# Pair 0's last two steps also with second layers of seven products, the change of form moved inside pair 0, its weight sets made first

## The chip, the cores and the metric

The kernel runs on one core of a Trainium2 chip. TensorE (PE) multiplies, VectorE (DVE) and ScalarE (ACT) read its results out of PSUM, GpSimd (POOL) works on SBUF alone, and SyncE (SP) issues most transfers. Each engine takes its own instructions strictly in the order of the program and waits for the others at semaphores. The metric is the time of one execution on the device in microseconds (us), the median of three runs.

## What is computed

The reference is a chain of a 2-D Fourier transform, a gated feed-forward layer, and a second feed-forward layer, "network two", which is where the change lies:

```python
def _moe2_ref(x, w_in, w_out):          # x: 12288 x 256, w_in: 256 x 2048, w_out: 2048 x 256
    h = x @ w_in
    g = h - np.tanh(h)
    return (g @ w_out).astype(np.float32)
```

## The kernel before

All products run in fp32r, with each operand split into a high part (a cast to fp32r, "hi") and a low part (the value minus its high part, "lo"). One product of a 128x128 weight block with 512 columns is three matmuls in a row (lines 395 to 397: high weights by high data, high weights by low data, low weights by high data).

Network two takes the tokens in 12 pairs (n) of 2x512 and w_in's columns in 8 steps (q) of 256; a step is written (n,q). Both layers of a step are 2x2 block products. The first layer is done with seven products instead of eight (operands `a11 a12 s1 s2 s3 s4 a22`, summed in banks `x`, `z`, `w`). Then come tanh, the subtraction, and the second layer. That layer has two forms. The whole form multiplies the four gated blocks 11, 12, 21, 22 by two halves of w_out, eight products (`WO`). The form of seven needs the same kind of sums on the gated data (`s1 s2 s3 s4`, made by DVE and POOL from `g11 g12 g22` and `x`) and of the weights (`W7`, seven blocks, a "set" for each q), but runs seven products: `a12 s4 a22` go straight into the output banks `o`, the others into a bank `k` whose sum is added into SBUF (`acc`).

`quad` writes a step with only whole forms; before, all of pair 0 goes through it. `step` writes a step of pairs 1 to 11, where q = 0, 1, 3, 4, 6, 7 have seven products and q = 2, 5 the whole form. How `step` orders its instructions depends on the two steps before it: form "c" if the last step was whole, "e" if the last was of seven and the one before it whole, "b" if both were of seven. The second layer of a step runs inside the next one or two steps, between their first-layer products. The low parts `a11`, `s2`, `s3`, `s4` and others are POOL's, and so are two of the sums (`+s2`: g22 - g11; `+s4`: g12 - g22).

Each step has four slots; `at(slot, ...)` puts side work into them and `fill` writes it out there. The side work around the change is: `weights2` (first-layer weight sets `TI` of pair 0 and `WO`), `seven` (the `W7` sets), `left2` (the next pair's left operands), `stream` (the later `TI`, reloaded from HBM). A `W7` set is made of one ACT cast of 384 columns, one POOL subtraction of 384 columns, four POOL subtractions of 128 (the first part), and, a few slots later, an ACT cast and a POOL subtraction of 512 columns (the second part).

Before, sets 0, 1, 3 are made in the last two steps of pair 0, set 4 in (1,2) and (1,3), set 6 in (1,5) and (1,6), set 7 in (1,6) and (1,7).

Of the kernel before, what the change touches and what calls it, by code (L numbers as in the profile page):

```python
# [375 lines left out]
NP = 12  # L376
# [30 lines left out]
class Kernel:  # L407
# [513 lines left out]
    def weights2(self, slot, q, pool, tag, bufs):  # L921
        a, b, out = [], [], []
        def load(to, pool, tag, bufs, i):
            def f():
                to.append(pool.tile([128, TOK], F32, tag=tag, name="wf", bufs=bufs))
                self.nc.sync.dma_start(out=to[-1], in_=self.wf[i])
            return f
        def ti():
            p, t = (self.p2a, f"TI{q}") if q < 4 else (self.w1, "T")
            self.TI[q] = p.tile([128, 2, 7, 128], F32R, tag=t, name="TI", bufs=1 if q < 4 else 4)  # L930
            f, g = self.quad_weights(self.p2a, self.TI[q])
            f(a[0])
            b.append(g)
            out.append(self.TI[q])
        def wo():
            p, t = (self.p2a, f"WO{q}") if q < 4 else (self.wvp, "wv")
            self.WO[q] = p.tile([128, 2, TOK], F32R, tag=t, name="WO", bufs=1 if q < 4 else 4)
            self.split(self.WO[q], b[1], self.V if q < 2 else self.G)
        def keep():
            self.nc.sync.dma_start(out=self.ti[q], in_=out[0].rearrange("p s k n -> p (s k n)").bitcast(F32))  # L940
        self.at(max(slot - 3, 16 * NP - 12), load(a, self.kp, "xt", 4, 4 + q))
        self.at(slot + 1, ti, None, None, None, lambda: b[0](None))
        self.at(16 * NP + ((5, 6, 10)[q] if q < 3 else 4 * q + 1), keep)
        self.at(slot + 4, load(b, pool, tag, bufs, 12 + q), None, wo)

    def seven(self, slot, q, pool, tag, bufs, src_pool, src_tag, src_bufs, t4):

        src, t = [], []
        def load():
            src.append(src_pool.tile([128, TOK], F32, tag=src_tag, name="wf", bufs=src_bufs))  # L950
            for to, at, n in ((0, 128, 128), (128, 0, 128), (256, 256, 256)):
                self.nc.sync.dma_start(out=src[0][:, to:to + n], in_=self.wf[12 + q, :, at:at + n])
        def first():
            self.W7[q] = pool.tile([128, 2, 7, 128], F32R, tag=tag, name="W7", bufs=bufs)
            f, g = self.quad_weights(t4(), self.W7[q])
            f(src[0])
            t.append(g)
        if q == 6:
            self.hook = first
        self.at(slot, *[first] * (q != 6), *[None] * (4 + (q == 6)), lambda: t[0](None))  # L960
        self.at(slot - (2 if q == 7 else 4), load)

# [13 lines left out]
    def sevens(self, n):  # L976

        return (0, 1, 3, 4, 6) if n == NP - 1 else (0, 1, 3, 4, 6, 7)

# [60 lines left out]

    def part(self, n, t, h, eng=None):

        if n == 0:
            a = self.room(self.p2b, "acc", "o", 7)
            (eng or self.V.tensor_copy)(a, self.C.pop((n, t, h)))
            return self.send(n, t, h, a)
# [13 lines left out]
    def whole_out(self, n, t, h):  # L1060

        if n == 0:
            return
        a = self.acc[n, t, h]
        self.G.tensor_add(a, a, self.acc[n, "t" if t else "s2"])
        self.send(n, t, h, a)

    def step(self, n, q):
# [26 lines left out]
        late = lambda *names: [p1["late"][k]() for k in names]  # L1095
        turn, end = (n, q) == (1, 0), (n, q) == (NP - 1, 7)
        new = lambda name: self.room(self.kp, "xt", name, 4)
# [5 lines left out]
        if two and self.last(p2["n"], p2["q"]) == p2["q"]:  # L1103
            g = group(p2, p3)
            k1, k2 = (lambda: self.apart(g, "s2")), (lambda *i: self.apart(g, "s3", *i))
        if 8 * n + q + 1 < 8 * NP:
            self.stream(8 * n + q + 1)
        self.odd ^= 1
        X, Z = self.bank(f"x{self.odd}", "x"), self.bank("z", "z")

        after = form == "b" and p1["form"] == "e" and (n, q) != (1, 5)
        if form == "b" and not after:
# [6 lines left out]
        if form == "b":  # L1119
            late("f22")  # L1120
            if (n, q) == (1, 5):
                self.hook()
            if after:
                late("L22", "s3")
            else:
                late("l22", "s3")
        elif form == "e":
            if (n, q) == (1, 1):
                late("f22", "L22", "c12", "g21")
            else:  # L1130
                late("l22", "c12", "f22", "g21")
        else:
            late("t21", "c12", "g21")
        A.copy(Z, X)  # L1134
        if form == "b":
            self.direct(p2, "s4")
            if (n, q) == (1, 2):
                self.direct(p2, "a22")
            if not after:
                self.direct(p1, "a22")  # L1140
            late("s1", "+s2", "hs1", "hs3", "c12", "t12")
        elif form == "c":
            self.whole(p1, "11", (1,))
            self.whole(p1, "22", (0,))
            late("t12", "h21", "g12")
            if q == 3 and n > 1:
                self.part(n - 1, 1, 1)
            late("l21", "h12")
        else:
            self.whole(p2, "21")  # L1150
            late("t12", "s3", "s1", "+s2")
            if end:
                late("hs1", "G12", "ls1")
            else:
                late("hs3", "ls3")
        P(Z, "a12")
        if form == "b":
            late("ls1", "ls3")
            if q == 1 and n > 1:
                C = self.C[n - 1, 0, 1]  # L1160
                V.tensor_add(C, C, self.acc[n - 1, "h"])
# [19 lines left out]
        if form == "b":  # L1181
            late("ha12", "+s4", "la12")
        if (n, q) == (1, 1):
            self.part(0, 1, 0)
            self.part(0, 1, 1, A.copy)
        self.fill()
        if form == "c":
            self.whole(p1, "22", (1,))
        elif form == "e":
            if (n, q) != (1, 1):  # L1190
                self.direct(p1, "a22")
            self.whole(p2, "12", (0,))
# [10 lines left out]
        add()  # L1203
        if q == 1 and n > 1:
            self.part(n - 1, 0, 0)
# [19 lines left out]
        elif form == "e":  # L1225
            self.whole(p2, "12", (1,))
        if (n, q) == (1, 1):
            self.part(0, 0, 0, A.copy)
        V.tensor_add(Z, Wb, s3)  # L1229
        if (n, q) == (1, 1):  # L1230
            self.part(0, 0, 1)
        if q == 1 and n > 1:
            self.outer(n - 1, 0, 1)
        if q == 0 and n > 1:
            self.part(n - 1, 1, 0)
# [255 lines left out]
```

## Time and profile before

| what | us |
|---|---|
| median of 3 runs (1611.01 to 1611.74) | 1611.54 |
| the profiled execution, its time | 1611.9 |
| its span, first to last instruction | 1610.1 |
| PE busy | 1595.5 |
| DVE, ACT, POOL busy | 1333.0, 1263.7, 1151.2 |

The span is what the trace shows of the execution; the rest of its time lies before the first and after the last instruction. Network two begins at 646.80 us, where the first product with `TI` starts. PE is drawn busy nearly all the time since matmuls overlap, so short waits show as starts that lie further apart than the matmuls alone would make them.

### The profile page before, as it was taken

How to read it: one execution, taken by the hardware profiler on the slowest of the kernel's cores; microseconds unless marked ns; L12 is line 12 of the kernel's file. 1: busy time of each engine (PE TensorE's matmuls, PEld its weight loads, DVE VectorE, ACT ScalarE, POOL GpSimd, SP SyncE). 2: the span in 40 equal slices, each digit the busy share in tenths (PEclk: the TensorE clock that was granted, in tenths of full speed). 3: DMA queues.
4: the chain of work that ended last, by engine and by line, in shares of the span. 5: the costliest groups of instructions: out<-in, count | busy, mean ns of one | idle time of the engine just before them, and what ended most of it. 6: DMA issues, size and time to landing. Idle time of an engine off the chain costs nothing.

```text
span 1610.1 us, 22467 instructions
## 1 busy us (share of the span) xinstructions
PE 1595.5 (99%) x7283; PEld 1305.2 (81%) x7283; DVE 1333.0 (83%) x2081; ACT 1263.7 (78%) x2444; POOL 1151.2 (71%) x962
## 2 busy tenths in 40 slices
PE   8999999999999999999999999999999999999998
PEld 7978888888888888787788888888888888888887
DVE  7987888888888887777787878887878787878787
ACT  5887777777777777788888888888787888888875
POOL 1156767656667676577887888787878787878764
PEclk9999999999999999999999999999999999999999
DMA  9630111112121112554142424343424242424240
GB/s 339 172 71 28 47 41 45 40 47 66 47 67 46 32 55 94 200 182 169 59 138 98 138 98 138 103 135 119 135 101 144 92 145 92 145 95 149 102 152 26
DMA packets 59349, 168.75 MB, mean 105 GB/s; under 512 B 6864, under 2 KB 15824, under 8 KB 59232
## 3 DMA queue, kind: packets, MB, share of 16 engines
q1 hardware_dynamic: 57648, 162.87, 29.7%
q0 software_dynamic: 1440, 4.46, 1.6%
q8 instruction: 57, 0.93, 0.2%
q14 instruction: 60, 0.49, 0.1%
q10 hardware_dynamic: 144, 0.00, 0.0%
HBM read 128.43 MB, written 38.86 MB: 104 GB/s over the span
## 4 chain that ended last, share of the span: by engine, by line
PE 93%; DVE 2%; DMA 1%; ACT 1%; POOL 1%; issue 1%; SPq 0%; DVEq 0%; ACTq 0%; POOLq 0%
PE o L395 11%; PE o L397 11%; PE o L396 11%; PE x L395 8%; PE x L397 8%; PE x L396 8%; PE w L395 4%; PE w L396 4%; PE w L397 4%; PE k L395 4%; PE k L396 4%; PE k L397 4%; PE z L395 2%; PE z L397 2%; PE z L396 2%; PE r L396 1%
## 5 line engine op out<-in xcount | busy, mean ns | idle before, releaser
L1094 POOL TENSOR_TENSOR s<-g,s 128x512 fp32r<-128x512 f32 x153 | 198.1, 1302 | 4.1 <-ACT s L1092 3.4
L696 POOL TENSOR_TENSOR s<-xk,s 128x512 fp32r<-128x512 f32 x94 | 125.1, 1332 | 87.8 <-ACT s L694 82.8
L696 POOL TENSOR_TENSOR a<-xk,a 128x512 fp32r<-128x512 f32 x70 | 92.3, 1327 | 121.2 <-ACT a L694 121.2
L396 PE MATMUL o<-m,wv 128*128 128x512 f32 x384 | 149.6, 390 | 0.1
L397 PE MATMUL o<-m,wv 128*128 128x512 f32 x384 | 149.5, 389 | 0.0
L395 PE MATMUL o<-m,wv 128*128 128x512 f32 x384 | 149.5, 389 | 0.0
L1094 POOL TENSOR_TENSOR a<-g,a 128x512 fp32r<-128x512 f32 x107 | 138.3, 1302 | 15.3 <-ACT g L1270 10.5
L1284 POOL TENSOR_TENSOR g<-g,g 128x512 f32<-128x512 f32 x65 | 84.3, 1297 | 53.4 <-DVE x L1283 42.5
L1087 ACT COPY s<-x 128x512 f32<-128x512 f32 x176 | 104.3, 593 | 22.6 <-PE x L397 19.6
L1083 ACT ACTIVATE c<-z 128x512 f32<-128x512 f32 x176 | 105.7, 601 | 10.1 <-DVE z L1229 8.2
L571 ACT ACTIVATE c<-z 128x512 f32<-128x512 f32 x112 | 67.3, 601 | 55.7 <-DVE z L660 54.9
L1243 DVE TENSOR_TENSOR z<-z,c 128x512 f32<-128x512 f32 x88 | 61.6, 700 | 52.1 <-ACT c L1083 49.5
L578 DVE TENSOR_TENSOR m<-z,m 128x512 fp32r<-128x512 f32 x112 | 76.8, 686 | 32.9 <-ACT m L576 32.9
L1092 ACT CAST s<-g 128x512 fp32r<-128x512 f32 x153 | 92.8, 623 | 5.6 <-DVE g L1283 5.6
L430 POOL TENSOR_TENSOR xr<-xt,xr 128x512 fp32r<-128x512 f32 x46 | 60.8, 1329 | 46.3 <-ACT xr L429 46.3
L576 ACT CAST m<-z 128x512 fp32r<-128x512 f32 x112 | 65.9, 589 | 27.9 <-DVE z L664 23.7
L396 PEld LDWEIGHTS o<-m,wv 128*128 128x128 f32 x384 | 72.1, 188 | 15.6 <-DVE m L578 0.5
L395 PEld LDWEIGHTS o<-m,wv 128*128 128x128 f32 x384 | 72.1, 188 | 15.2
L397 PEld LDWEIGHTS o<-m,wv 128*128 128x128 f32 x384 | 72.1, 188 | 15.1
L1134 ACT COPY z<-x 128x512 f32<-128x512 f32 x88 | 50.2, 570 | 39.7 <-PE x L397 37.7
L1229 DVE TENSOR_TENSOR z<-w,s 128x512 f32<-128x512 f32 x88 | 61.5, 699 | 22.9 <-PE w L397 15.8
L395 PE MATMUL w<-s,TI 128*128 128x512 f32 x192 | 77.4, 403 | 0.0
(1027 smaller groups left out, 5915.3 us busy)
## 6 DMA issues: line engine op xcount, KB each, us to landing
TI<-ti SPq DMA_DIRECT2D x88, 896.0 KB, 4.8
spill<-r SPq DMA_DIRECT2D x48, 256.0 KB, 2.6
xk<-spill SPq DMA_DIRECT2D x48, 256.0 KB, 6.3
out<-o SPq DMA_DIRECT2D x45, 256.0 KB, 2.0
ti<-TI SPq DMA_DIRECT2D x8, 896.0 KB, 5.1
wf<-wf SPq DMA_DIRECT2D x17, 256.0 KB, 3.0
raw<-w_in SPq DMA_DIRECT2D x32, 128.0 KB, 2.2
cv<-w_out SPq DMA_DIRECT2D x16, 256.0 KB, 3.1
```

The source lines that it names most:

```text
L395: T.matmul(ps, w[0], m[0], start=start, stop=False, skip_group_check=True)
L396: T.matmul(ps, w[0], m[1], start=False, stop=False, skip_group_check=True)
L397: T.matmul(ps, w[1], m[0], start=False, stop=stop, skip_group_check=True)
L571: A.activation(t, src, ACT.Tanh if ph == 2 else ACT.Relu)
L576: A.copy(M[blk][:, 0], g)
L578: V.tensor_sub(M[blk][:, 1], g, M[blk][:, 0].bitcast(F32))
L696: eng.tensor_sub(S[name][:, 1], src(), S[name][:, 0].bitcast(F32))
L1083: A.activation(t, src, TANH)
L1087: A.copy(t, src)
L1092: A.copy(M[k][:, 0], src)
L1094: eng.tensor_sub(M[k][:, 1], src, M[k][:, 0].bitcast(F32))
L1284: "+s2": lambda: G.tensor_sub(g("22"), g("22"), g("11")), "+s4": plus4,
```

## The change

Steps (0,6) and (0,7) are now written by `step` with seven products in the second layer; pair 0's other six steps stay in `quad`. The change of form, which stood at (1,0), stands at (0,6). From (1,0) on all steps have the order that pairs 2 to 11 have. Pair 0's results no longer leave by four copies but by the additions that the other pairs have. `WO` 6 and 7 are not made ahead any more. The six `W7` sets are the same, but are made in the order 6, 7, 0, 1, 3, 4 and at other slots: sets 6 and 7 in steps (0,4) to (0,6), set 0 from the end of (0,6) through (0,7), set 1 from the end of (0,7), set 3 in (1,1) and (1,2), set 4 in (1,2) and (1,3). The `TI` sets of pair 0 are made one to five slots earlier.

```diff
         self.at(max(slot - 3, 16 * NP - 12), load(a, self.kp, "xt", 4, 4 + q))
-        self.at(slot + 1, ti, None, None, None, lambda: b[0](None))
-        self.at(16 * NP + ((5, 6, 10)[q] if q < 3 else 4 * q + 1), keep)
-        self.at(slot + 4, load(b, pool, tag, bufs, 12 + q), None, wo)
+        self.at(slot + 1, ti, None, None, lambda: b[0](None))
+        self.at(16 * NP + ((5, 6, 10)[q] if q < 3 else 3 * q + 1), keep)
+        if q < 6:
+            self.at(slot + 4, load(b, pool, tag, bufs, 12 + q), None, wo)
...
-        if q == 6:
-            self.hook = first
-        self.at(slot, *[first] * (q != 6), *[None] * (4 + (q == 6)), lambda: t[0](None))
-        self.at(slot - (2 if q == 7 else 4), load)
+        self.at(slot, first, None, None, lambda: t[0](None))
+        self.at(slot - (3 if q in (0, 1) else 4), load)
...
-        return (0, 1, 3, 4, 6) if n == NP - 1 else (0, 1, 3, 4, 6, 7)
+        return (6, 7) if n == 0 else (0, 1, 3, 4, 6) if n == NP - 1 else (0, 1, 3, 4, 6, 7)
...
-        turn, end = (n, q) == (1, 0), (n, q) == (NP - 1, 7)
+        turn, end = (n, q) == (0, 6), (n, q) == (NP - 1, 7)
...
-            if (n, q) == (1, 1):
+            if (n, q) == (0, 7):
                 late("f22", "L22", "c12", "g21")
...
-            if (n, q) != (1, 1):
-                self.direct(p1, "a22")
+            self.direct(p1, "a22")
...
-            self.weights2(z0 + 4 * (j - 2), j, self.kp, "xt", 4)
+            self.weights2(z0 + 3 * j - 6, j, self.kp, "xt", 4)
...
-        for i, (q, slot, src) in enumerate(((0, 23, xt), (1, 26, xt), (3, 28, xt), (4, 40, wf), (6, 51, wf), (7, 55, wf))):
-            self.seven(z0 + slot, q, *((self.p2a, f"TI{i}", 1) if i < 4 else ring), *src, t4[i % 2])
+        for i, (q, slot, src) in enumerate(((6, 19, xt), (7, 23, wf), (0, 27, wf), (1, 31, wf), (3, 37, wf), (4, 42, wf))):
+            self.seven(z0 + slot, q, *((self.p2a, f"TI{i - 2}", 1) if i > 1 else ring), *src, t4[i % 2])
...
-                if n:
+                if (n, q) == (0, 6):
+                    self.pend["seven"] = False
+                    self.C.update({(0, t, h): self.O[t][h] for t in range(2) for h in range(2)})
+                if 8 * n + q > 5:
                     self.step(n, q)
```

First place: POOL, from the last step of pair 0 into pair 1. Before, in (0,7) and (1,0), it makes `W7` sets (7244 is set 0, 7329 set 1, 7400 set 3; a row with `wf` and the four with `t4` are a first part) and has one low part to make:

```order
L430 TENSOR_TENSOR W7_7400<-wf_7297,W7_7400 128x384
L516 TENSOR_TENSOR t4_7401<-wf_7297 128x128
L517 TENSOR_TENSOR t4_7401<-wf_7297 128x128
L518 TENSOR_TENSOR t4_7401<-wf_7297,t4_7401 128x128
L519 TENSOR_TENSOR t4_7401<-wf_7297,t4_7401 128x128
L430 TENSOR_TENSOR W7_7329<-t4_7330,W7_7329 128x512
L1094 TENSOR_TENSOR a11_7500<-g11_7498,a11_7500 128x512
L430 TENSOR_TENSOR W7_7400<-t4_7401,W7_7400 128x512
```

Only one row of the steps' own work, `a11`, stands among them. Now, in (0,7) and (1,0), from `+s2` of (0,6) to the low part of `a22` of (0,7) (7339 is set 0, 7443 set 1):

```order
L1265 TENSOR_TENSOR g22_7357<-g22_7357,g11_7312 128x512
L1087 TENSOR_TENSOR s3_7374<-g11_7312,s3_7374 128x512
L1087 TENSOR_TENSOR a11_7405<-g11_7388,a11_7405 128x512
L1087 TENSOR_TENSOR s4_7416<-g12_7393,s4_7416 128x512
L1087 TENSOR_TENSOR s2_7419<-g22_7357,s2_7419 128x512
L430 TENSOR_TENSOR W7_7339<-t4_7340,W7_7339 128x512
L430 TENSOR_TENSOR W7_7443<-wf_7395,W7_7443 128x384
L516 TENSOR_TENSOR t4_7444<-wf_7395 128x128
L517 TENSOR_TENSOR t4_7444<-wf_7395 128x128
L518 TENSOR_TENSOR t4_7444<-wf_7395,t4_7444 128x128
L519 TENSOR_TENSOR t4_7444<-wf_7395,t4_7444 128x128
L1087 TENSOR_TENSOR a22_7440<-g22_7464,a22_7440 128x512
```

The sets of pair 0's end stood among few low parts; set 0's end and set 1's first part now stand between the low parts of two steps.

Second place: POOL up to `+s4` (L1279 before, L1260 now) in (1,2). Before, from the low part of `a22` in (1,1):

```order
L1094 TENSOR_TENSOR a22_7523<-g22_7535,a22_7523 128x512
L1284 TENSOR_TENSOR g22_7535<-g22_7535,g11_7498 128x512
L1094 TENSOR_TENSOR s3_7552<-g11_7498,s3_7552 128x512
L1094 TENSOR_TENSOR a11_7584<-g11_7566,a11_7584 128x512
L1094 TENSOR_TENSOR s4_7595<-g12_7571,s4_7595 128x512
L1094 TENSOR_TENSOR s2_7598<-g22_7535,s2_7598 128x512
L1094 TENSOR_TENSOR a22_7623<-g22_7642,a22_7623 128x512
L1284 TENSOR_TENSOR g22_7642<-g22_7642,g11_7566 128x512
L1094 TENSOR_TENSOR s3_7659<-g11_7566,s3_7659 128x512
L1279 TENSOR_TENSOR s_7680<-g12_7669,g22_7642 128x512
```

All ten rows are the steps' own work. Now the twelve rows that end with `+s4` in (1,2) (7641 is set 3):

```order
L1087 TENSOR_TENSOR a11_7623<-g11_7621,a11_7623 128x512
L1087 TENSOR_TENSOR s4_7635<-s_7611,s4_7635 128x512
L1087 TENSOR_TENSOR s2_7638<-g22_7696,s2_7638 128x512
L430 TENSOR_TENSOR W7_7641<-wf_7528,W7_7641 128x384
L516 TENSOR_TENSOR t4_7642<-wf_7528 128x128
L517 TENSOR_TENSOR t4_7642<-wf_7528 128x128
L518 TENSOR_TENSOR t4_7642<-wf_7528,t4_7642 128x128
L519 TENSOR_TENSOR t4_7642<-wf_7528,t4_7642 128x128
L1058 TENSOR_TENSOR o_7540<-o_7540,acc_7677 128x512
L1265 TENSOR_TENSOR g22_7696<-g22_7696,g11_7621 128x512
L1087 TENSOR_TENSOR s3_7712<-g11_7621,s3_7712 128x512
L1260 TENSOR_TENSOR s_7733<-g12_7722,g22_7696 128x512
```

Set 3's first part now stands ahead of that `+s4`; before, no set did.

Third place: ACT at the start of the step after the change of form. Before, at (1,1):

```order
L1083 ACTIVATE c_7520<-x_7457 128x512
L1092 CAST a22_7523<-z_7458 128x512
L1270 COPY g22_7535<-z_7458 128x512
L1134 COPY z_7531<-x_7530 128x512
L1083 ACTIVATE c_7547<-w_7510 128x512
```

There the high part of `a22` is followed by the copies into `g22` and `z` at once. Now, at (0,7):

```order
L1076 ACTIVATE c_7334<-x_7267 128x512
L1085 CAST a22_7337<-z_7268 128x512
L429 CAST W7_7339<-wf_7305 128x384
L1251 COPY g22_7357<-z_7268 128x512
L1125 COPY z_7353<-x_7352 128x512
```

Set 0's first cast has come between the high part of `a22` and the two copies.

## Rows read from the trace of the kernel before

**Rows 1.** The page: busy times, and the chain that ended last.

```profile
PE 1595.5 (99%) x7283; PEld 1305.2 (81%) x7283; DVE 1333.0 (83%) x2081; ACT 1263.7 (78%) x2444; POOL 1151.2 (71%) x962
...
PE 93%; DVE 2%; DMA 1%; ACT 1%; POOL 1%; issue 1%; SPq 0%; DVEq 0%; ACTq 0%; POOLq 0%
```

**Rows 2.** Windows: bounds, length, busy time of each engine, granted clock, DMA.

```profile
837.87:916.58 78.71, 78.71 (x344) 63.56 (x343) 64.90 (x102) 64.89 (x122) 64.70 (x52) 1.00 0.36 121
878.48:916.58 38.10, 38.10 (x167) 30.59 (x166) 32.82 (x52) 32.13 (x61) 34.45 (x28) 1.00 0.44 146
916.58:927.53 10.95, 10.95 (x50) 8.93 (x48) 8.73 (x14) 8.07 (x16) 6.17 (x6) 1.00 0.24 84
```

**Rows 3.** Timeline of PE: first matmuls of (0,6), (1,0), (1,1), (1,5), (2,7), (3,3).

```profile
709.22 0.39 PE L395 MATMUL x<-a,TI 128*128 128x512 f32 x1
...
730.30 0.39 PE L395 MATMUL x<-a,TI 128*128 128x512 f32 x1
...
737.95 0.40 PE L395 MATMUL x<-a,TI 128*128 128x512 f32 x1
...
777.58 0.39 PE L395 MATMUL x<-a,TI 128*128 128x512 f32 x1
...
878.48 0.39 PE L395 MATMUL x<-a,TI 128*128 128x512 f32 x1
...
916.58 0.39 PE L395 MATMUL x<-a,TI 128*128 128x512 f32 x1
```

**Rows 4.** Timeline of POOL from (2,7) to (3,2); in brackets idle before, releaser.

```profile
881.46 1.29 POOL L1284 TENSOR_TENSOR g<-g,g 128x512 f32<-128x512 f32 x1 [2.22 <-DVE x L1283]
...
888.36 1.29 POOL L1094 TENSOR_TENSOR a<-g,a 128x512 fp32r<-128x512 f32 x1 [0.46 <-ACT g L1270]
...
899.39 1.30 POOL L1284 TENSOR_TENSOR g<-g,g 128x512 f32<-128x512 f32 x1 [0.81 <-DVE x L1283]
...
911.98 1.29 POOL L1279 TENSOR_TENSOR s<-g,g 128x512 f32<-128x512 f32 x1
```

**Rows 5.** The chain in order of time, steps (1,5) to (1,6): start, us, what.

```profile
778.26 0.42 ACT W L429
778.75 1.01 POOL W L430
...
781.56 1.11 POOL g L1284
...
784.01 1.32 POOL s L1279
785.36 1.14 ACT s L1092 x2
...
787.03 0.70 DVE z L1243
787.73 0.60 DVE acc L1034
788.37 0.50 PE x L395
```

**Rows 6.** The chain in order of time, start of (1,1).

```profile
738.50 0.36 ACT a L1092
738.98 0.60 ACT g L1270
739.61 0.58 ACT z L1134
740.23 0.50 PE z L395
```

**Rows 7.** Timeline of PE: a wait in the Fourier phase.

```profile
40.68 1.13 PE L192 MATMUL s<-f,fe 128*128 128x128 f32 x8 [1.87 <-DVE fe L169]
```

**Rows 8.** The window behind that wait, columns as in rows 2.

```profile
42.00:44.00 2.00, 2.00 (x12) 2.00 (x11) 2.00 (x5) 1.30 (x5) 0.00 (x0) 0.51 1.00 265
```

More of the change, by code (lines that the diff above doesn't have):

```diff
@@ L937, in wo @@
             self.WO[q] = p.tile([128, 2, TOK], F32R, tag=t, name="WO", bufs=1 if q < 4 else 4)
-            self.split(self.WO[q], b[1], self.V if q < 2 else self.G)
+            self.split(self.WO[q], b[-1], self.V if q < 2 else self.G)
         def keep():
@@ L1039, in send, with part @@
         f() if now else self.at(self.now + 1, f)
[L1041 to L1046, printed above, removed]
+    def part(self, n, t, h):
         s = self.acc[n, "h" if h else "a11"]
@@ L1060, in whole_out @@
     def whole_out(self, n, t, h):
-        if n == 0:
-            return
         a = self.acc[n, t, h]
@@ L1105, in step @@
             k1, k2 = (lambda: self.apart(g, "s2")), (lambda *i: self.apart(g, "s3", *i))
-        if 8 * n + q + 1 < 8 * NP:
+        if 8 <= 8 * n + q + 1 < 8 * NP:
             self.stream(8 * n + q + 1)
@@ L1109, in step @@
         X, Z = self.bank(f"x{self.odd}", "x"), self.bank("z", "z")
-        after = form == "b" and p1["form"] == "e" and (n, q) != (1, 5)
+        after = form == "b" and p1["form"] == "e"
         if form == "b" and not after:
@@ L1120, in step @@
             late("f22")
-            if (n, q) == (1, 5):
-                self.hook()
             if after:
@@ L1136, in step @@
             self.direct(p2, "s4")
-            if (n, q) == (1, 2):
-                self.direct(p2, "a22")
             if not after:
@@ L1145, in step @@
             late("t12", "h21", "g12")
-            if q == 3 and n > 1:
+            if q == 3 and n:
                 self.part(n - 1, 1, 1)
@@ L1158, in step @@
             late("ls1", "ls3")
-            if q == 1 and n > 1:
+            if q == 1 and n:
                 C = self.C[n - 1, 0, 1]
@@ L1168, in step @@
         t11 = bend(Z)
-        side = seven and (form == "e" or q < 2)
+        side = seven and (form == "e" or q < 2 or turn)
         def gate():
@@ L1182, in step @@
             late("ha12", "+s4", "la12")
-        if (n, q) == (1, 1):
-            self.part(0, 1, 0)
-            self.part(0, 1, 1, A.copy)
         self.fill()
@@ L1203, in step @@
         add()
-        if q == 1 and n > 1:
+        if q == 1 and n:
             self.part(n - 1, 0, 0)
@@ L1226, in step @@
             self.whole(p2, "12", (1,))
-        if (n, q) == (1, 1):
-            self.part(0, 0, 0, A.copy)
         V.tensor_add(Z, Wb, s3)
-        if (n, q) == (1, 1):
-            self.part(0, 0, 1)
-        if q == 1 and n > 1:
+        if q == 1 and n:
             self.outer(n - 1, 0, 1)
-        if q == 0 and n > 1:
+        if q == 0 and n:
             self.part(n - 1, 1, 0)
@@ L1247, in step @@
             V.tensor_sub(X, X, st["t21"])
-        if q == 1 and n > 1:
+        if q == 1 and n:
             self.whole_out(n - 1, 1, 0)
@@ L1251, in step @@
             lo("22", Z, V)
-        if q == 3 and n > 1:
+        if q == 3 and n:
             self.whole_out(n - 1, 1, 1)
@@ L1305, in phase2 @@
         self.W7, self.C, self.acc, self.older, self.oldest = {}, {}, {}, None, None
-        self.at(z0 + 28, lambda: self.stream(8))
         self.TI = dict(enumerate(self.TI))
         for j in range(3, 8):
-            self.weights2(z0 + 4 * (j - 2), j, self.kp, "xt", 4)
+            self.weights2(z0 + 3 * j - 6, j, self.kp, "xt", 4)
         xt, wf, ring = (self.kp, "xt", 4), (self.p2a, "wf", 1), (self.w1, "T", 4)
         t4 = (lambda: self.p2b, lambda: self.p2a)
-        for i, (q, slot, src) in enumerate(((0, 23, xt), (1, 26, xt), (3, 28, xt), (4, 40, wf), (6, 51, wf), (7, 55, wf))):
-            self.seven(z0 + slot, q, *((self.p2a, f"TI{i}", 1) if i < 4 else ring), *src, t4[i % 2])
+        for i, (q, slot, src) in enumerate(((6, 19, xt), (7, 23, wf), (0, 27, wf), (1, 31, wf), (3, 37, wf), (4, 42, wf))):
+            self.seven(z0 + slot, q, *((self.p2a, f"TI{i - 2}", 1) if i > 1 else ring), *src, t4[i % 2])
         for n in range(NP):
@@ L1319, in phase2 @@
                     self.homes = [[self.p2a, "WO0", 1, 1.5], [self.p2a, "WO1", 1, 2.5], [self.p2a, "WO3", 1, 4.5], [self.w1, "WR", 1, 0.], [self.p2b, "M", 2, 1.], [self.p2b, "M", 2, 1.1],
-                                  [self.wvp, "wv", 4, 5.6], [self.wvp, "wv", 4, 7.6], [self.wvp, "wv", 4, 9.8]] + [[self.act, "m", 4, t] for t in (8.3, 8.6, 9.3, 9.8)]
+                                  [self.wvp, "wv", 4, 5.6], [self.wvp, "wv", 4, 1.2], [self.wvp, "wv", 4, 1.3]] + [[self.act, "m", 4, t] for t in (6.3, 6.6, 7.3, 7.8)]
                 if q == 1 and n + 1 < NP:
@@ L1334, in phase2 @@
                     self.at(self.now + 1, *self.plain(7))
-            if n == 0:
-                self.pend["seven"] = False
-                self.C.update({(0, t, h): self.O[t][h] for t in range(2) for h in range(2)})
         p, w, n, G = self.pend, self.older, NP - 1, self.G
```

## The prediction

> **What bounds the kernel now.** I read the page first. PE is busy for 99% of the span and holds 93% of the chain that ended last [rows 1]: time is matmuls, plus the waits between them. The reader should then see how small those waits are. From the start of (0,6) to that of (1,0) PE takes 730.30 - 709.22 = 21.08 us [rows 3] for 45 + 48 matmuls, 0.2267 each, without a wait. A settled pair, (2,3) to (3,3), takes 78.71 us [rows 2] for 342 matmuls, which alone would be 77.53. So waits are 1.2 us per pair. Next I looked for the engine that PE would wait for. Over a settled pair POOL is busy 64.70 of 78.71 us [rows 2], which looks like room. The timeline shows that the room lies in one place. From (2,7) to (3,2) POOL runs from 881.46 to 911.98 + 1.29 = 913.27 in 24 rows of 128x512, one every 1.26 us (ten steps from 899.39 to 911.98), with two idle spells of 0.46 and 0.81 us [rows 4]; its rest comes in (n,3), where it is busy 6.17 of 10.95 us [rows 2], and in (n,6). This run ends in `+s4` of (3,2), and the wait it can cause is seen in (1,5) [rows 5]: there `+s4` ends at 784.01 + 1.32 = 785.33, ACT casts it and its neighbour, does the tanh, DVE the subtraction and the drain of bank `k`, and only then may PE begin (1,6) at 788.37, 3.04 us behind POOL. In the settled pair the same distance is 916.58 - 913.27 = 3.31 [rows 3, 4]. So the run from (n,7) to (n,2) has little over one microsecond to give before PE waits.
>
> **What the change takes away.** By the order of instructions PE has six matmuls fewer: 6 x 0.2267 = 1.36 us. The four copies of pair 0's results go, which PE did not wait for by themselves. The irregular order of pair 1 goes too. What that is worth I take from marks, as if POOL were no matter. (0,5) ends with one product that used to stand behind the mark, so (0,6) begins at 709.22 + 3 x 0.2267 = 709.90. Its matmuls are those of the old (1,0), 30 of them, with the same waits for ACT, so it takes the old 737.95 - 730.30 = 7.65 [rows 3]; (0,7) begins at 717.55. From there the form is that of (2,7) on: 38.10 us to (1,3) and 78.71 more to (2,3) [rows 2], at 834.36. Before, (2,3) begins at 837.87 [rows 2]. By matmuls and waits of PE's own the change therefore gives 3.5 us: 1.36 for six matmuls, the rest for the irregular waits of pair 1, set 6's in (1,5) among them.
>
> **What it adds on POOL.** The run from (n,7) to (n,2) now also exists in pair 0 and 1, and weight sets stand in it. I price a set by the one of rows 5: ACT's first cast 0.42 (it holds the queue some 0.5), POOL's first part 781.56 - 778.75 = 2.8, the second part one row of 1.25, as in rows 4.
>
> *Where the run starts.* In (2,7) `+s2` starts 881.46 - 878.48 = 2.98 us into the step [rows 3, 4]. In (0,7) POOL must first make set 0's first part, whose cast stands behind the high part of `a22`. At the old change of form that high part was cast at 738.50, 0.55 into the step [rows 6]; with 0.5 for it and 0.45 for set 0's cast, POOL starts at 1.5 and is through at 4.3. The low part of `a22` follows there on POOL, to 5.55. So `+s2` comes 5.55 into the step, 2.6 later than settled. The same cast delays the copy into `z`, for which PE waited at the old place already [rows 6], by another 0.5; that wait is taken up by the longer one.
>
> *What stands in it.* By the order, the same 24 rows, plus the second part of set 0, all of set 1 and the first part of set 3: 1.25 + 2.8 + 1.25 + 2.8 = 8.1 us. The 24 rows took 913.27 - 881.46 = 31.81, of which 1.27 idle: 30.5 without.
>
> *Its end.* 5.55 + 30.5 + 8.1 = 44.15 us into (0,7). With the 3.04 of rows 5 PE starts (1,3) at 47.2, where matmuls alone would have had it at 38.10: **9.1 us of new waits**, spread over (0,7) to (1,2). I expect about 1 at `a22` of (0,6) in (0,7), some 3 at `a22` of (0,7) in (1,0), whose low part stands behind set 1's first part, and over 3 at the start of (1,3).
>
> *What has cover.* Set 3's second part and set 4 (1.25 + 4.05 us) fall mostly into (1,3), where POOL is idle for 10.95 - 6.17 = 4.8 us [rows 2]. What is left over reaches (1,4), where the row ahead of `+s2` runs back to back: from 0 to 1.25 us, and I take 0.3. Sets 6 and 7 in pair 0 have `TI` buffers as homes that PE reads until a step's last matmul, so ACT now waits for PE twice; behind it stand a left operand's cast, the tanh and the copy of `x`, four operations of some 0.5, and PE comes to need that copy four products (2.7 us) on. From 0 to 0.7 us; I take 0. The earlier `TI` sets of pair 0 put up to three casts between ACT's steps; no row shows a wait there, and with 0 to 0.5 I take 0.
>
> **The sum.** (1,3) begins at 717.55 + 47.2 = 764.75, (2,3) at 764.75 + 78.71 + 0.3 = 843.8, before at 837.87: **+5.9 us**. All later steps have the order of before. The profiled execution took 1611.9 (0.4 above the median of the runs shown), which would be 1617.8, with a span of 1616.0; the median goes from 1611.54 to **1617.4**.
>
> **A rule on the clock.** After PE had waited 1.87 us in the Fourier phase [rows 7], the next window shows a granted clock of 0.51 [rows 8], the 1.2 GHz level; in the windows of network two above it is 1.00 [rows 2]. The Trainium skill, "TensorE: Matmul & The Clock Gate", section "Why this matters for your kernels", advises against idle gaps of TensorE between bursts of matmuls, since one can put it back to the lower clock. That speaks against this change, whose waits would be longer than the one in rows 7; the sum above goes by the full clock.
>
> **Rivals.**
> *POOL's run is hidden (faster).* If the low parts can come 9 us later without PE noticing, the 3.5 us of the marks stand: 1608.0. For it speaks POOL's 18% of idle time over a pair. Against it stand rows 5, where one first part ahead of `+s4` already ended in a wait of PE. It decides itself at `+s4` of (1,2): hidden if that ends 35 us into (0,7), not 44.
>
> *Each set costs what set 6 cost.* (1,5) with set 6's first part took 788.37 - 777.58 = 10.79 us [rows 3, 5] for 42 matmuls, 9.52: 1.3 of waits, half of the set's 2.8, the rest having been slack. If the sets here find such slack each time, three first parts cost 3.9, against the 3.5: +0.4, 1611.9. Against it: the slack is there once per run, not once per set.
>
> *The clock falls as well.* If the wait of some 3 us ahead of (1,3) does what that of rows 7 did, PE runs at half speed for a while: at 0.51 the 2 us of rows 8 lose 1 us. I take one to two such windows, for one or two waits: 1 to 3 us more, 1618.5 to 1620.5.
>
> *The change does not do what it says.* The order shows six matmuls fewer and all sets made before their first use, so this has no chance of its own.
>
> **Chances and range.** POOL's run as priced, 1615.5 to 1619: 0.62. With a fall of the clock: 0.13. Price per set, 1611 to 1614.5: 0.14. Hidden: 0.11. 0.2% of the time is 3.2 us, about what a measurement can tell from no change. Slower by more than that is above 1614.8: 0.62 + 0.13 less 0.01 = 0.74; faster (below 1608.3) 0.11; the same 0.15. The range takes in the first three, with the unknown costs above (up to 0.95 + 0.7 + 0.5) at its upper end, and leaves out the hidden case and the worst of the clock: 1611.0 to 1620.5. The likeliest case alone spans 1615.5 to 1619.
>
> **What would show it.** In the profile after: POOL without idle from about 719 us to the end of `+s4` in (1,2) near 761.7; PE's longest waits in (1,0) and at the start of (1,3), the latter behind DVE's drain of `k`; (0,7) starting near 717.5, (2,3) near 843.8; network two with 4143 matmuls. Were (1,3) to begin before 758, the run was not the bound, and I would be wrong at the step that adds the sets to POOL's 30.5 us; were (0,7) to begin past 718.5, pair 0's sets cost what I took as nothing.

## The result, and the profile after

| | before | after |
|---|---|---|
| median of the runs, us | 1611.64 (1611.01 to 1611.82) | 1621.93 (1621.01 to 1623.0) |
| ratio, 95% interval | | 1.0065 [1.0047, 1.0082] |
| profiled execution, its span, us | 1611.9, 1610.1 | 1623.0, 1621.2 |

The kernel is 10.3 us slower; 1617.4 was forecast, with 1620.5 as the upper end. The sign and the place were right, the size was not. The page after, in the two parts that answer to [rows 1]: TensorE is still busy 99% of the span, but what GpSimd, VectorE, ScalarE and DMA hold of the chain that ended last has grown.

```profile
PE 1598.1 (99%) x7277; PEld 1305.6 (81%) x7277; DVE 1335.4 (82%) x2085; ACT 1265.7 (78%) x2448; POOL 1169.4 (72%) x977
...
PE 89%; POOL 3%; DVE 3%; ACT 2%; DMA 2%; issue 1%; SPq 0%; DVEq 0%; ACTq 0%; POOLq 0%
```

Windows after, columns as in [rows 2]: (0,7) up to (1,3), the first 5.37 us of (1,3), (1,3) up to (2,3), and (2,3) up to (3,3).

```profile
718.36:766.80 48.44, 40.31 (x167) 30.11 (x165) 34.60 (x55) 36.12 (x70) 47.59 (x47) 0.98 0.35 114
766.80:772.17 5.37, 5.37 (x13) 4.20 (x14) 3.09 (x6) 2.15 (x4) 3.24 (x6) 0.50 0.81 324
766.80:848.96 82.16, 81.29 (x342) 65.56 (x343) 63.91 (x101) 65.33 (x122) 68.64 (x58) 0.97 0.35 126
848.96:927.67 78.71, 78.71 (x343) 63.57 (x342) 64.97 (x102) 64.94 (x122) 64.62 (x52) 1.00 0.36 121
```

The last row is the settled pair of [rows 2] to the hundredth, so all of the loss lies ahead of (2,3). The first row took 38.10 us in a settled pair and takes 48.44; GpSimd is busy for 47.59 of them. The second row is the surprise: 13 matmuls in 5.37 us, at a granted clock of 0.50, the 1.2 GHz level. What TensorE waited for from (0,7) to (1,4) (window 715 to 795 us: total, number of waits, longest):

```profile
PE x L395 <- DMA TI<-ti: 3.5, 1, 3.5
PE o L396 <- POOL a L1087: 3.3, 2, 2.2
PE z L395 <- ACT z L1125: 1.0, 2, 0.6
PE w L395 <- DVE g L1257: 0.9, 1, 0.9
PE k L395 <- DVE s L1087: 0.2, 1, 0.2
```

The second row is the wait for the low part of `a22` in (0,7) and (1,0), 1.1 and 2.2 us, where about 1 and some 3 were forecast. The first stands at the start of (1,3). There `+s4`, VectorE's drain of `k` and the product appear in the timeline like this:

```profile
761.16 1.30 POOL L1260 TENSOR_TENSOR s<-g,g 128x512 f32<-128x512 f32 x1
...
764.77 0.68 DVE L1031 COPY acc<-k 128x512 f32<-128x512 f32 x1
...
766.80 0.76 PE L395 MATMUL x<-a,TI 128*128 128x512 f32 x1 [3.46 <-DMA TI<-ti]
```

`+s4` ends at 762.46, 44.10 us into (0,7), where 44.15 was forecast, and the drain at 765.45, 2.99 behind it. The product begins 1.35 us later still, because its `TI` has not landed. SyncE's queue shows why:

```profile
742.05 0.32 SPq L1281 DMA_DIRECT2D TI<-ti  x1
757.48 1.27 SPq L953 DMA_DIRECT2D wf<-wf  x3
758.84 0.85 SPq L1037 DMA_DIRECT2D out<-o  x2
759.74 0.47 SPq L1281 DMA_DIRECT2D TI<-ti  x1
760.25 2.92 SPq L916 DMA_DIRECT2D xk<-spill  x4
```

The load of set 4 goes into the one buffer of `wf`, which GpSimd read for set 3 until 757.4; SyncE's queue is served in order and stood there for 15 us, with the stream of (1,3) behind it.

### The profile page after: what moved, and what is told of

It reads as the page before. It is cut to its first block, busy times and chain, and to the rows that moved or that the text cites. A ratio compares the mean times of both kernels' runs of the same rounds, so it can differ in the third digit from the quotient of the medians.

```text
span 1621.2 us, 22478 instructions
## 1 busy us (share of the span) xinstructions
PE 1598.1 (99%) x7277; PEld 1305.6 (81%) x7277; DVE 1335.4 (82%) x2085; ACT 1265.7 (78%) x2448; POOL 1169.4 (72%) x977
## 4 chain that ended last, share of the span: by engine, by line
PE 89%; POOL 3%; DVE 3%; ACT 2%; DMA 2%; issue 1%; SPq 0%; DVEq 0%; ACTq 0%; POOLq 0%
PE o L395 11%; PE o L397 11%; PE o L396 10%; PE x L395 8%; PE x L397 7%; PE x L396 7%; PE w L395 4%; PE w L397 4%; PE w L396 4%; PE k L395 4%; PE k L396 4%; PE k L397 4%; PE z L395 2%; PE z L397 2%; PE z L396 2%
## 5 line engine op out<-in xcount | busy, mean ns | idle before, releaser
L1087 POOL TENSOR_TENSOR s<-g,s 128x512 fp32r<-128x512 f32 x157 | 203.7, 1305 | 4.1 <-ACT s L1085 3.2
L1087 POOL TENSOR_TENSOR a<-g,a 128x512 fp32r<-128x512 f32 x112 | 144.7, 1303 | 10.3 <-ACT g L1251 8.7
L395 PE MATMUL k<-s,W 128*128 128x512 f32 x200 | 79.1, 396 | 0.2 <-DVE s L1087 0.2
```

The source lines that it names most:

```text
L395: T.matmul(ps, w[0], m[0], start=start, stop=False, skip_group_check=True)
L1087: eng.tensor_sub(M[k][:, 1], src, M[k][:, 0].bitcast(F32))
```

## The experiments

Three theories. **A**, the prediction's: the weight sets stand in GpSimd's in-order run from `+s2` in (0,7) to `+s4` in (1,2), and TensorE pays what the run exceeds its slack by. **B**: the form itself in pair 0, with its seven products, costs. **C**: SyncE's queue, hence the late stream, is the main cause. A set is described below as (number, slot of its first part, slot of its load, buffer, home, engine); a step has four slots, so slot 28 is the first of (0,7), 40 the first of (1,2), just behind `+s4`. All runs side by side; "+s4" is its end and "(1,3)" the start of that step, both from the start of (0,7), and the last two columns are lengths, all in us of the profiled execution. These four columns come from one execution each, so they need not add up to the medians. In no34 and ring_early3 it was the longest of the runs (1618.02 and 1620.06 us), and network two began at 649.84 and 648.66 us there, some 2 and 3 us later than in the others.

| run | median | ratio to before, 95% | +s4 | (1,3) | (1,3) to (2,3) | (0,0) to (0,7) |
|---|---|---|---|---|---|---|
| after | 1621.93 | 1.0065 [1.0047, 1.0082] | 44.1 | 48.4 | 82.2 | 71.2 |
| no_sets | 1609.57 | 0.9984 [0.9975, 0.9992] | 35.2 | 38.6 | 78.8 | 71.2 |
| no34 | 1616.06 | 1.0025 [1.0015, 1.0035] | 41.3 | 44.4 | 78.7 | 71.2 |
| load4_late | 1623.56 | 1.0071 [1.0058, 1.0084] | 44.7 | 47.7 | 84.3 | 71.2 |
| late34 | 1622.22 | 1.0063 [1.0051, 1.0076] | 41.9 | 45.2 | 84.5 | 71.2 |
| early67 | 1626.90 | 1.0093 [1.0077, 1.0108] | 35.2 | 38.6 | 84.3 | 82.6 |
| ring67v | 1624.56 | 1.0075 [1.0061, 1.0089] | 35.3 | 38.6 | 84.8 | 79.9 |
| ring67g | 1623.84 | 1.0070 [1.0057, 1.0082] | 35.3 | 38.6 | 84.5 | 79.8 |
| ring_load | 1620.35 | 1.0053 [1.0041, 1.0066] | 35.2 | 38.5 | 84.4 | 77.0 |
| ring_early3 | 1617.57 | 1.0029 [1.0017, 1.0042] | 35.6 | 38.9 | 79.6 | 78.9 |
| ring_late2 | 1613.73 | 1.0011 [1.0002, 1.0020] | 38.0 | 41.3 | 79.5 | 72.0 |
| ring_hook | 1613.53 | 1.0013 [1.0004, 1.0022] | 35.6 | 38.9 | 79.4 | 74.4 |

**no_sets** and **no34**: the sets not made.

```
-        for i, (q, slot, src) in enumerate(((6, 19, xt), (7, 23, wf), (0, 27, wf), (1, 31, wf), (3, 37, wf), (4, 42, wf))):
+        for i, (q, slot, src) in enumerate(((6, 19, xt), (7, 23, wf))):
...
+            if q == 6:
+                self.W7.update({k: self.W7[6] for k in (0, 1, 3, 4)})
```

no34 keeps (0, 27) and (1, 31) and replaces only 3 and 4. It and the runs from early67 to ring_early3 also put the `t4` of all sets into one buffer, where the changed kernel alternates between two.

> Sets 0, 1, 3 and 4 are not made or loaded; set 6 stands in for them, so the results of pairs 1 to 11 are others, with every matmul of the changed kernel kept. Theory A (the prediction: the weight sets stand in GpSimd's run between `+s2` in (0,7) and `+s4` in (1,2), and TensorE waits for that run; the late stream of (1,3) and the fall of the clock only follow from it): the run is 24 rows as in a settled pair, (1,3) begins 38 to 39 us after (0,7), the clock stays, 1608 to 1609.5 us. Theory B (the seven products and the change of form in pair 0 cost by themselves, in ScalarE and VectorE): no less than 1615. Theory C (SyncE's queue: set 4's load held the stream of (1,3) back, and the rest is small): the DMA's 1.3 us and the fall's 2.5 go, the waits in (0,7) and (1,0) stay, 1617 to 1618.5.

> Sets 3 and 4 are not made; set 6 stands in for them, so the results of pairs 1 to 11 are others. Sets 0 and 1 keep their places. Theory A (GpSimd's run): 2.8 us less in the run, which ends 41.3 us into (0,7); with 3.04 behind it (1,3) begins 44.3 to 44.6 into (0,7), against 38.6 without the four sets, and (1,3), (1,4) lose nothing: 1609.6 + 5.8 = 1615.4, plus 1.7 for each fall of the clock behind a wait of 2 us or more (one is likely, in (1,0)): 1615 to 1617.5. Price per set (1.3 for each first part that stands there): 1612.2. Theory C (the late stream and set 4's load are the whole loss): 1609.6 to 1611.

Without the four sets TensorE waits once from (0,7) to (1,4), for 0.2 us, and the two windows (0,7) to (1,3), (1,3) to (2,3) are those of a settled pair to half a microsecond:

```profile
PE z L395 <- ACT z L1127: 0.2, 1, 0.2
```

```profile
717.91:756.47 38.56, 38.37 (x167) 30.59 (x166) 33.26 (x53) 33.02 (x63) 36.27 (x29) 1.00 0.44 144
756.47:835.26 78.79, 78.79 (x343) 63.58 (x342) 64.94 (x102) 64.85 (x122) 64.65 (x52) 1.00 0.36 121
```

B is out: without the four sets the new form takes 2.5 us less than the kernel before (3.5 was forecast from the marks), and the sets cost 1621.93 - 1609.57 = 12.4. This run takes the sets' casts on ScalarE and their loads away too, so it does not yet say which part of them costs; doses, below, adds rows on GpSimd alone. no34 fits A in place and price: `+s4` at 41.3 (41.3 expected), (1,3) at 44.4 (44.3 to 44.6), 1616.06 us. So sets 0 and 1 cost 6.5 us by themselves and the price per set (1612.2) is out, as is C (1609.6 to 1611).

**load4_late** and **late34**: sets 3 and 4 later.

```
-(3, 37, 33, wf, 2, G), (4, 42, 38, wf, 3, G)
+(3, 37, 33, wf, 2, G), (4, 45, 41, wf, 3, G)     load4_late
+(3, 40, 36, wf, 2, G), (4, 44, 41, wf, 3, G)     late34
```

> Only set 4 moves: its load from slot 38 to slot 41 (behind the stream of (1,3) in SyncE's queue), its two parts from slots 42 and 45 to 45 and 48. Theory A: `+s4` of (1,2) ends where it did (44 us into (0,7)), (1,3) begins 1.3 us earlier, with VectorE's drain of `k` as what ends the wait of about 2.1 us; if that shorter wait spares the clock, 2.5 us more: 1618 to 1620.6. Theory C: all of the wait ahead of (1,3) goes, and the fall: 1615.5 to 1617. Theory B: no change, 1621.9.

> Set 3's parts move from slots 37 and 40 to 40 and 43 (behind `+s4` of (1,2)), set 4's from 42 and 45 to 44 and 47, its load to 41. Theory A: 2.8 us less in GpSimd's run, `+s4` ends 41 to 41.5 us into (0,7), (1,3) begins 2.8 + 1.3 us earlier after a wait under 1.5 us, and the clock does not fall; (1,4) may lose 1 us to set 4: 1614.5 to 1617.5. Theory C: as load4_late with its wait gone, 1615.5 to 1617, but with `+s4` without influence on where (1,3) begins. Theory B: 1621.9.

The waits of load4_late from 715 to 795 us:

```profile
PE o L396 <- POOL a L1087: 3.4, 2, 2.2
PE w L395 <- DVE g L1257: 2.3, 1, 2.3
PE x L395 <- DVE acc L1031: 1.9, 1, 1.9
PE z L395 <- ACT z L1125: 1.0, 2, 0.6
```

The DMA is gone from the list and the drain of `k` now ends the wait ahead of (1,3), at 1.9 us where A said 2.1; C's claim that all of it goes is false. Yet the total did not fall, 1623.56 us against A's 1618 to 1620.6: set 4, moved, delayed `+s2` of (1,4) (2.3 us instead of 0.9), and the clock fell behind each of the three longest waits, as these windows show:

```profile
735.82:739.24 3.42, 3.42 (x9) 2.64 (x9) 0.07 (x1) 0.00 (x0) 3.42 (x3) 0.50 0.19 55
766.54:769.96 3.42, 3.42 (x10) 2.65 (x9) 3.09 (x7) 2.15 (x4) 1.21 (x1) 0.50 0.15 63
787.02:790.44 3.42, 3.42 (x10) 2.68 (x9) 1.40 (x2) 1.42 (x3) 3.42 (x3) 0.50 0.00 0
```

late34 took `+s4` to 41.9 and (1,3) to 45.2, near what A expected, and lost it one step on, which A had put at 1 us, so that its 1622.22 us missed A's 1614.5 to 1617.5:

```profile
PE w L395 <- DVE g L1257: 3.2, 1, 3.2
```

GpSimd's timeline before that wait: set 4's second part and the left operands' rows run back to back up to `+s2` (third row), for which VectorE's `g` waits.

```profile
779.86 1.29 POOL L430 TENSOR_TENSOR W<-t,W 128x512 fp32r<-128x512 f32 x1
781.11 1.26 POOL L706 TENSOR_TENSOR xk<-xk 128x512 f32<-128x512 f32 x1
782.33 1.25 POOL L1265 TENSOR_TENSOR g<-g,g 128x512 f32<-128x512 f32 x1
```

So (1,3) has no room for two sets; ring_early3, below, has one there.

**doses**: the changed kernel with idle work on GpSimd, to price its run in settled pairs.

```
+        def rows(m):
+            t, w = self.p2b.tile([128, 4, 128], F32, tag="t4", name="t4"), self.W7[0]
+            for _ in range(m):
+                self.G.tensor_sub(t, w[:, 0, 0:4].bitcast(F32), w[:, 1, 0:4].bitcast(F32))
+        for n, m in ((3, 1), (4, 2), (5, 3), (6, 4), (8, 6), (10, 8)):
+            self.at(z0 + 32 * n + 1, lambda m=m: rows(m))
```

> The changed kernel with rows of 128x512 added on GpSimd (1.26 us each, into a spare tile, read by nobody) at the second filling place of (n,0): 1 row in pair 3, 2 in pair 4, 3 in pair 5, 4 in pair 6, 6 in pair 8, 8 in pair 10. Theory A (TensorE waits for what GpSimd's run exceeds its slack by, 1.27 us of idle in it and 0.3 at its end): 0, 1.0, 2.2, 3.5, 6.0 and 8.5 us, 21 in all, the most in one or two waits from (n,0) to (n,3); and 1.7 us more for each wait of 2 us or longer that brings the clock down for 3.41 us: 1643 to 1652. Price per set (half of what is added, as in (1,5) of before): 15 us in all, 1637, without a part that costs nothing. Theory C (it was SyncE's queue): nothing but what reaches the streams, under 5 us: below 1627.

It took 1652.09 us, ratio 1.0254 [1.0240, 1.0268]. Windows (n,0) up to (n,4), columns as before, for 1, 2, 3, 4, 6 and 8 rows, and last for none (pair 9):

```profile
896.42:937.27 40.85, 40.85 (x178) 32.84 (x177) 34.62 (x55) 32.53 (x62) 35.63 (x29) 1.00 0.41 136
975.32:1017.49 42.17, 41.14 (x178) 32.75 (x177) 34.63 (x55) 32.55 (x62) 36.91 (x30) 1.00 0.39 132
1055.55:1099.05 43.50, 41.46 (x178) 32.69 (x177) 34.65 (x55) 32.56 (x62) 38.16 (x31) 1.00 0.38 127
1137.08:1183.97 46.89, 43.83 (x178) 34.63 (x177) 34.72 (x55) 32.65 (x62) 39.45 (x32) 0.93 0.36 118
1300.73:1349.11 48.38, 42.84 (x178) 34.02 (x177) 34.71 (x55) 32.66 (x62) 41.90 (x34) 0.93 0.33 114
1465.88:1518.33 52.45, 44.26 (x178) 35.00 (x177) 34.70 (x55) 32.67 (x62) 44.47 (x36) 0.90 0.31 106
1387.16:1427.80 40.64, 40.64 (x178) 32.91 (x177) 34.63 (x55) 32.47 (x62) 34.44 (x28) 1.00 0.41 136
```

Against 40.64 that is +0.2, +1.5, +2.9, +6.3, +7.7 and +11.8 us. The first row is nearly free, the next two cost 1.3 each, a whole row; from four on the clock column falls as well. In the pairs with a clock of 1.00 theory A's 0, 1.0, 2.2 is 0.2 to 0.7 low: two rows are 2.52 us and cost 1.53, so the slack is 1.0 us, not the 1.57 (1.27 + 0.3) put there. The total lies at the upper end of A's 1643 to 1652 and far from the price per set (1637) and C (below 1627). Since nothing but GpSimd's rows was added, its run alone is enough to make TensorE wait.

**Sets made early**: seven attempts to keep what no_sets shows. early67 makes 6 and 7 in the homes of `TI0` and `TI1`, on VectorE; the others put 6 and 7 into the ring of `T` and `TI7` (in ring67 and ring_load `TI6` too) into a home that is free.

```
+(6, 9, 5, wf, 0, V), (7, 13, 10, wf, 1, V), (0, 19, 15, xt, None, G), (1, 23, 19, wf, None, G), (3, 40, 36, wf, 2, G), (4, 44, 41, wf, 3, G)      early67
+(6, 4, 1, wf, None, G), (7, 8, 5, wf, None, G), (0, 19, 15, xt, 2, G), (1, 23, 19, wf, 3, G), (3, 40, 36, wf, 0, G), (4, 44, 41, wf, 1, G)       ring67g; ring67v: set 4 with V
+(6, 4, 1, wf, None, G), (7, 12, 9, wf, None, G), (0, 19, 16, wf, 2, G), (1, 23, 20, wf, 3, G), (3, 40, 36, wf, 0, G), (4, 44, 41, wf, 1, G)      ring_load
+(6, 4, 1, wf, None, G), (7, 12, 9, wf, None, G), (0, 16, 13, wf, 2, G), (1, 20, 17, wf, 3, G), (3, 24, 21, wf, 0, G), (4, 40, 36, wf, 1, G)      ring_early3
+(6, 4, 1, wf, None, G), (7, 12, 9, wf, None, G), (0, 17, 14, wf, 2, G), (3, 22, 18, wf, 0, G), (1, 24, 20, xt, 3, G), (4, 40, 36, wf, 1, G)      ring_late2, second part at + 4
```

> Sets 6 and 7 are made in (0,2) to (0,4), with their subtractions on VectorE, in the buffers of `TI0` and `TI1`; sets 0 and 1 take their places at slots 19 and 23 on GpSimd; sets 3 and 4 as in late34. Nothing of a set is left between `+s2` of (0,7) and `+s4` of (1,2). Theory A: the run is hidden, (1,3) begins 38 to 39.5 us after (0,7), no fall of the clock; (1,3) and (1,4) may lose up to 1.5 us to sets 3 and 4, pair 0 up to 1 to VectorE: 1608 to 1611. Theories B and C: the waits of (0,7) and (1,0) stay, 1615 or more.

> Sets 6 and 7 are made in (0,1) and (0,2) on GpSimd, where it idles 5.5 us, in two buffers of the ring of `T`; `TI6` and `TI7` take the homes of `TI0` and `TI1`; sets 0 and 1 come at slots 19 and 23, set 3 at 40 and 43 behind `+s4`, set 4 at 44 and 47 with its subtractions on VectorE. Nothing of a set stands between `+s2` of (0,7) and `+s4` of (1,2). Theory A: (0,7) to (1,3) as without the sets (38.6 us), pair 0 up to 1.5 us longer as GpSimd is full there, (1,3) and (1,4) up to 2: 1609.6 to 1613. Theory B or C: 1615 or more, with waits in (0,7) and (1,0).

> As ring67v, with set 4's subtractions on GpSimd. Theory A: the same up to (1,3); there GpSimd has 4.8 us of idle time for 8.1 us of sets 3 and 4, so `+s2` of (1,4) comes 3.3 us late and (1,4) waits 3 to 5 us, as in late34, with a fall of the clock behind it: 1613 to 1617. If GpSimd's row is not what (1,4) waits for, it is as fast as ring67v.

In all three `+s4` comes at 35.2 to 35.3 and (1,3) at 38.6, as without the sets: A's mechanism holds again. The totals miss, since the cost went elsewhere. In early67 pair 0 became 11.4 us longer: above all, VectorE's `z` in (0,3) stood behind set 7's pieces (a wait of 4.5 us, with a fall of the clock). In ring67g, one wait of 6.6 us in (0,2) for ScalarE; SyncE's queue and ScalarE's timeline there:

```profile
659.75 0.45 SPq L940 DMA_DIRECT2D ti<-TI  x1
670.76 1.27 SPq L953 DMA_DIRECT2D wf<-wf  x3
672.07 1.85 SPq L916 DMA_DIRECT2D xk<-spill  x4
```

```profile
670.76 0.62 ACT L429 CAST W<-t 128x512 fp32r<-128x512 f32 x1 [1.16 <-POOL t L519]
676.10 0.62 ACT L694 CAST a<-xk 128x512 fp32r<-128x512 f32 x1 [4.72 <-DMA xk<-spill]
```

The same trap as in (1,2) of the changed kernel: set 7's load stood at slot 5 until set 6 had been read out of the one `wf` buffer, and the left operands' loads stood behind it.

> As ring67g, but set 7's load leaves slot 5, where SyncE's queue stood at it until GpSimd had read set 6 out of the one buffer of `wf` (670.76) with the left operands' loads behind it, for slot 9, and its parts stand at 12 and 15. If that queue made the wait of 6.3 us in (0,2) and the fall of the clock behind it: 8 to 8.7 us less than ring67g, 1615 to 1616.5, with (1,3) and (1,4) losing 6 us to sets 3 and 4 as there. If GpSimd's new sets themselves made it: 1620 or more.

Theory C's mechanism, then, is real, but here too only part: with the load moved (set 0's load and its buffer moved as well) the wait in (0,2) shrank from 6.6 to 1.8 us, another of 3.0 stood in (0,5), and the run took 1620.35, just inside the second case, that of GpSimd's sets themselves. These remaining waits have the bracket of the first ScalarE row above: the cast of the second part of a weight set (a `W7` in (0,2), a `TI` in (0,5)) stands at the head of ScalarE's in-order queue until GpSimd's last subtraction `L519` is done.

> Set 6 at slot 4, 7 at 12, 0 at 16, 1 at 20, 3 at 24, all of them before (0,7), set 4 alone behind `+s4` (40 and 43); `TI6` is made at 19 and 22 in the ring, `TI7` at 13 and 16 in the home of `TI1`. Theory A: (0,7) to (1,4) as without the sets, and set 4's 4.05 us in the 4.8 us that GpSimd idles in (1,3); pair 0 has 16.2 us of sets where it had 10.9, with 6.7 us of idle: up to 3 us of waits there. 1609.6 to 1613. Theory B: 1615 or more. If set 4 alone already costs (1,3) and (1,4) what sets 3 and 4 cost together in ring67g: 1615.

> As ring_early3, but each set's second part comes four filling places behind its first, no longer three (so that ScalarE's cast of it, which stood 1.2 to 2.5 us at the head of ScalarE's queue waiting for GpSimd's last subtraction, finds that done), and sets 0, 3 and 1 begin at slots 17, 22 and 24, set 1 from a load at 20. If those waits of ScalarE made the 3.5 us in (0,2) and the 4.1 in (0,5): 1610 to 1612.5. If GpSimd is simply overfull in pair 0, the waits come back a step later, and what is left over delays `+s2` of (0,7): 1615 to 1618.

ring_early3 shows what set 4 alone costs in (1,3) and (1,4): 79.6 against 78.8. Its 1617.57 us miss A's 1609.6 to 1613, as pair 0 lost 7.7 us in its trace where up to 3 were expected. It still had waits of ScalarE of that kind in (0,2) and (0,5), seen in its timeline:

```profile
672.80 0.62 ACT L429 CAST W<-t 128x512 fp32r<-128x512 f32 x1 [1.17 <-POOL t L519]
...
708.03 0.62 ACT L429 CAST W<-t 128x512 fp32r<-128x512 f32 x1 [1.79 <-POOL t L519]
```

With second parts one filling place later, and sets 0, 3 and 1 at other slots, ring_late2 has pair 0 at 72.0 against 78.9 us and no fall of the clock in network two: the waits for ScalarE are gone from its list. Its 1613.73 us lie between the two cases, though, and a lateness came up in (0,7) to (1,2): `+s4` at 38.0, and a wait of 1.5 us for the low part of `a22`. Whether GpSimd had one set's worth too much is what ring_hook asks.

> As ring_late2, but set 6's first part is written at the very start of (0,1), where GpSimd idled 5.5 us (658.7 to 664.2 in ring_late2, as ScalarE's next cast for it stands far down in the step), its second at slot 4; 7, 0, 3 and 1 move up to slots 10, 15, 20 and 23. If what is left of the waits in (0,6) to (1,1) (3.3 us more than without the four sets) comes from GpSimd being late by these 4.05 us: they go, 1610 to 1611.5, no slower than before. If ScalarE's casts among the steps' own work, not GpSimd, make them: 1613 to 1614.5.

```
-            self.at(slot, first, None, None, None, lambda: t[0](None))          set 6 only
+            self.hook = first                                                   called at the start of (0,1)
```

ring_hook's waits from 660 to 800 us:

```profile
PE x L395 <- ACT s L593: 1.8, 1, 1.8
PE w L395 <- DVE g L1259: 0.6, 1, 0.6
PE z L395 <- ACT z L1127: 0.6, 1, 0.6
```

(1,3) is back at 38.9, so GpSimd was late by that set, but 1.8 us appeared in (0,4): 1613.53, the second case of its expectation in size, though not where it was expected. It recovers 8.4 of the 12.4 us and is not faster than the kernel before; no run with all sets was. What ends the wait in (0,4) the trace shows, first the chain that ended last, then ScalarE's timeline:

```profile
684.79 0.47 POOL t L519
...
685.28 0.32 SPq L953
...
687.07 0.43 SPq L926
```

```profile
691.99 0.62 ACT L429 CAST WO<-wf 128x512 fp32r<-128x512 f32 x1 [2.88 <-DMA wf<-wf]
693.41 0.57 ACT L593 COPY s<-x 128x512 f32<-128x512 f32 x1
```

It is the trap of SyncE's queue once more: a set's load (L953) stood there until GpSimd's last subtraction had read the `wf` buffer, the load of a piece of `WO` (L926) stood behind it, and ScalarE sat idle for 2.88 us until that piece had landed, with the copy that TensorE needed (L593) behind its cast of that piece. No run moved that load.

## Why the prediction was right, and where it was wrong

*Taken away.* The forecast of 3.5 us by marks was 2.5 in no_sets; the 1.0 missing is 0.5 in pair 0, taken as nothing though bounded, and 0.46 from (0,7) to (1,3) (38.56 against 38.10).

*Added on GpSimd.* Right: the run's length, its end (44.10 against 44.15) and the distance to the drain. (1,3) should have begun 47.2 us into (0,7); it began at 48.44. The step that failed there is "*What stands in it*": it counted the sets' rows on GpSimd and not their loads on SyncE. Set 4's load held the stream back; the missing term is 1.24 us. In load4_late, where the stream is on time, (1,3) begins 3.04 us behind the end of `+s4`, just the forecast distance; in the changed kernel it is 4.34.

*What has cover.* From (1,3) to (2,3) 78.71 + 0.3 was forecast and 82.16 measured. Of the 3.15 us, the window of 13 matmuls at 0.50 gives 5.37 - 13 x 0.2267 = 2.4. The rest, 0.7, is the wait for `+s2` of (1,4), mis-sized in "what is left over reaches (1,4), [...] I take 0.3": its row was 0.9 us.

*The clock.* This is the largest miss, 2.4 us. "The sum above goes by the full clock" was wrong, and "With a fall of the clock: 0.13" too low, for a row of the trace before already showed a 1.87 us wait followed by a fall [rows 7, 8] and 3 us was forecast at two places. The rival's size, 1 to 3 us, was right; added to 1617.4, the 2.4 give 1619.8, still inside the range, which failed only with the other terms on top. The Trainium skill, "TensorE: Matmul & The Clock Gate", section "Why this matters for your kernels", advises against idle gaps between bursts of matmuls, as one can bring back the lower clock. The trace agrees, with 0.50 behind the 3.46 us wait.

The ledger in the profiled execution: pair 0 0.45, the DMA 1.24, (1,3) and (1,4) 3.15, together 4.8 us above the forecast from the start of network two to (2,3); that start itself was 0.4 us late (647.16 against 646.80), which makes the 5.2 between 1617.8 and 1623.0. The range ended too low because it "leaves out [...] the worst of the clock" and knew nothing of the stream.

*The rivals.* Hidden: refuted, as `+s4` ended at 44, though no_sets shows that its 1608.0 was near what the change without its sets gives. Price per set: refuted by no34 and doses; there is slack once, 1.0 us, and behind it the second and the third row cost a row each.

## What to carry to other kernels

Price work added to an in-order engine by its place in that engine's run, not by the engine's idle share: here one row was nearly free and the second and third cost their full 1.3 us each. List with it every load that it needs and ask what stands behind that load in its queue; a load into a single buffer holds the queue until the last reader of that buffer is done, which cost 1.2 us here and most of a 6.6 us wait in ring67g. Where a wait of TensorE is forecast that is as long as one that the trace shows with a fall of the clock behind it, give the fall a term in the sum, with its chance, and do not leave it to a rival alone.

## What the runs showed of the hardware

The same wait does not always bring the clock down. Five kernels with the same work up to there (after, no34, load4_late, late34, doses) had a wait of 2.2 us in (1,0); the clock fell behind it in three (load4_late, late34, doses), for 3.4 us each, and in two it did not. Here the window behind it in no34, and then in late34:

```profile
738.45:741.87 3.42, 3.42 (x15) 2.85 (x16) 0.69 (x1) 0.59 (x1) 3.40 (x3) 1.00 0.00 0
```

```profile
737.27:740.69 3.42, 3.42 (x10) 2.67 (x9) 0.69 (x1) 0.88 (x2) 3.42 (x3) 0.50 0.00 0
```

Five matmuls fewer in 3.42 us, at 0.2267 each, are 1.1 us. In network two it fell behind every wait of 3.1 us and more that these runs show; behind one of 3.0 in ring_load it did not, and behind one of 1.9 in load4_late it did. What decides stays open.

VectorE's rows can grow beside GpSimd's. In early67 a 128x128 subtraction of two SBUF operands took 0.28 us on VectorE while GpSimd stood idle, and 1.07 and 0.54 while it ran rows:

```profile
678.04 0.28 DVE L516 TENSOR_TENSOR t<-wf 128x128 f32<-128x128 f32 x1
...
692.84 1.07 DVE L516 TENSOR_TENSOR t<-wf 128x128 f32<-128x128 f32 x1
693.83 0.54 DVE L517 TENSOR_TENSOR t<-wf 128x128 f32<-128x128 f32 x1
```

The Trainium skill, "SBUF — State Buffer", section "Who interferes with whom", says that a VectorE instruction with two SBUF inputs contends with a GpSimd one that reads SBUF. These rows agree; no run tests it alone. The four subtractions together took 2.45 us there (692.84 to 695.29) and 1.0 beside an idle GpSimd, and `z`, for which TensorE waited 4.5 us in (0,3), came right behind them.
